# The first 128 positions of a sparse attention, computed on 64-key ranges, with the division on GpSimd

## The chip, the cores and the metric

The kernel runs on one core of a Trainium2 chip. Its engines work side by side and each in its own order: TensorE (PE, matrix products and transposes; PEld is its loading of weights), VectorE (DVE), ScalarE (ACT), GpSimd (POOL) and SyncE (SP). SP, ACT and POOL can issue DMA transfers, which 16 DMA engines carry out. Sums of PE land in PSUM, which has eight banks; all else is in SBUF. The metric is the time of one execution on the device in microseconds, the median of several runs.

## The reference

```python
# q, k, v: (4, 8, 576, 64)
scores = scale * np.matmul(q, k.transpose(0, 1, 3, 2))
rel = pos[:, None] - pos[None, :]
mask_local = (rel >= 0) & (rel < 32)
mask_strided = (rel >= 0) & (pos[None, :] % 32 == pos[:, None] % 32)
# heads 0 to 3 take mask_local, heads 4 to 7 mask_strided
attn = softmax(np.where(mask, scores, -1e9))        # sum + 1e-9 in the divisor
x = (attn @ v).transpose(0, 2, 1, 3).reshape(2304, 512)
h = np.maximum(x @ w_in, 0.0)                        # w_in (512, 2048)
x = (s * h * h + b) @ w_out                          # w_out (2048, 512)
out = ((x @ w_a) * (x @ w_b)) @ w_o2                 # d_ff 1536
```

The weights arrive as 64-bit floats. The kernel reads them as pairs of 32-bit words, builds 32-bit floats from them, and splits each into a high and a low half for PE.

## The kernel before

The work is one attention and two MLPs. The 2304 tokens are taken in five blocks. Block 0 has the first 128 positions of all four batch entries, 512 columns; blocks 1 to 4 have the other positions of one batch entry each. For each block the first MLP runs through 16 slices of its inner width: `h_mm` (12 matmuls, written `h`) and, two slices later, `o_mm` (12 matmuls, `acc`). During block n the attention of block n + 1 is computed in small steps between the slices (`plan`, `attend`), in four `local` and two `strided` pieces.

The first positions have nothing to hide behind. The class `First` computes them for one batch entry each, and the string `ORDER` interleaves the steps of the four by hand. In a step's name the last digit is the batch entry. `Tq` and `Tk` transpose q and k (`fps`), `qe` and `ke` copy them out, `S` makes the scores (`fss`): for each head a full 128x128 product, with the mask added by a matmul. `m1`, `m0`, `nb`, `su`, `e1`, `e0`, `sm_` and `rc` make maxima, exponentials, sums and reciprocals. `P1`, `P0` transpose the probabilities (`fpp`), `p1`, `p0` copy them out, `V` multiplies with v (`fpo`), `no` divides, `X` transposes the result (`fpx`), and `hi` and `lo` split it into the two halves of x. The steps `c1`, `d0`, `d1`, `d2`, `ch`, `cl` convert the first two slices of `w_in`; the digit says which. `W` issues weight loads, and `I8` lets PE run eight matmuls of a filler, `lull` (as `idle(8)` does at the start).

PE's instructions are issued in the order of the program (`in_order`), and so are those of ACT and DVE in this part (`act`, `dve`). SP's queue has all loads but two: q and k of the four entries, v, the first weights, s and b, and then the q and k of the first local piece (`qk`, lines 281 to 285), of the strided ones (`sqk`) and so on. A load takes one of eight semaphores in turn, so it is issued when the load eight places before it has landed. Piece 0 of `local` starts at step -5, so its transposes (`pst`, line 291) stand on PE right ahead of the first `h`:

```python
if n == 1:
    near[0] = (0, near[0][1], (-5, -3, 0, 1, 1, 2, 3))
...
for number in (-5, -4, -3):
    attend(number)
```

GpSimd makes the masks: those of the first positions (`first_mask`, `fmask`) and those of the later pieces (`late_masks`, `mwork`).

Of the kernel before, what the change touches and what calls it, by code (L numbers as in the profile page):

```python
# [8 lines left out]
F32 = mybir.dt.float32  # L9
F32R = mybir.dt.float32r  # L10
U32 = mybir.dt.uint32
BF16 = mybir.dt.bfloat16
# [6 lines left out]
P = 128  # L19
# [6 lines left out]
def sparse_attention_two_mlps(  # L26
# [44 lines left out]
    ps_acc = ctx.enter_context(tc.tile_pool(name="ps_acc", bufs=4, space=PSUM))  # L71
    ps_h = ctx.enter_context(tc.tile_pool(name="ps_h", bufs=1, space=PSUM))
    ps_a = ctx.enter_context(tc.tile_pool(name="ps_a", bufs=3, space=PSUM))

# [478 lines left out]

    def slot(pool, shape, name, dtype=F32):
        return pool.tile(shape, dtype, tag="w", name=name)

    def first_mask():
        m = slot(wpa, [P, 2 * TF + TF], "fmask")
        m_b = m[:, 2 * TF:].bitcast(BF16)
        m = m[:, 0:2 * TF].rearrange("p (i c) -> p i c", i=2)  # L560
# [3 lines left out]
        nc.gpsimd.affine_select(  # L564
            out=m[:, 0], in_=m[:, 0], compare_op=ALU.is_ge, fill=NEG, base=0,
            pattern=[[-1, TF]], channel_multiplier=1,
        )
        nc.gpsimd.affine_select(
            out=m[:, 0], in_=m[:, 0], compare_op=ALU.is_gt, fill=NEG, base=STR,
            pattern=[[1, TF]], channel_multiplier=-1,  # L570
        )
        for i in range(TF // STR):
            nc.gpsimd.affine_select(
                out=m[:, 1], in_=m[:, 1], compare_op=ALU.not_equal, fill=0.0, base=-i * STR,
                pattern=[[-1, TF]], channel_multiplier=1,
            )
        m_b = m_b.rearrange("p (i c) -> p i c", i=2)
        nc.vector.tensor_copy(out=m_b, in_=m)
        return m_b
# [3 lines left out]

    def idle(number):
        for _ in range(number):
# [17 lines left out]

    class First:
        def __init__(self, bb, qk, vn, m_b, pool, tag):
            self.bb, self.qk, self.vn, self.m_b = bb, qk, vn, m_b
            self.bank = lambda shape, name: pool.tile(shape, F32, tag=tag, name=name)
            self.ps = {}

        def columns(self, e):  # L610
            if e == 0:
                self.qkT = slot(wpb, [P, 2, HP, TF], "fqkT")
            ps = self.ps["T", e] = self.bank([P, HP, TF], "fps")
            for pair in range(HP):
                mm_t(ps[:, pair], self.qk[:, e, 2 * pair:2 * pair + 2].rearrange("p h d -> p (h d)"), ident)
# [10 lines left out]
        def ke(self):  # L626
            if self.bb % 2:
                act(out=self.qkT[:, 1], in_=self.ps["T", 1], func=AF.Copy)
            else:
                dve("tensor_copy", out=self.qkT[:, 1], in_=self.ps["T", 1])  # L630

        def S(self):
            self.pt = slot(wpa, [P, 2, HP, TF], "fpt")
            self.mx = lp.tile([P, 2, HP], F32, tag="fmx", name="mx", bufs=2)
            self.sm = lp.tile([P, 2, HP], F32, tag="fsm", name="sm", bufs=4)
            for a in (1, 0):
                ps = self.ps["S", a] = self.bank([P, HP, TF], "fss")
                mm(
                    ps.rearrange("p (i j) c -> p i j c", i=2), lhsT=ident_b,
                    rhs=self.m_b[:, :, None, :].to_broadcast([P, 2, HP // 2, TF]), start=True, stop=False,  # L640
                )
            for pair in range(HP):
                for a in range(2):
                    qT, kT = (self.qkT[a * D:(a + 1) * D, e, pair] for e in range(2))
                    mm(self.ps["S", a][:, pair], lhsT=qT, rhs=kT, start=False, stop=(pair == HP - 1))

        def top(self, a):
            dve("tensor_reduce", out=self.mx[:, a], in_=self.ps["S", a], op=ALU.max, axis=AX.X)

        def m1(self):  # L650
            self.top(1)

        def m0(self):
            self.top(0)

        def nb(self):
            dve("tensor_scalar_mul", out=self.mx[:, 1], in0=self.mx[:, 1], scalar1=-scale)

        def su(self):
            dve(  # L660
                "tensor_tensor", out=self.pt[:, 0], in0=self.ps["S", 0],
                in1=self.mx[:, 0, :, None].to_broadcast([P, HP, TF]), op=ALU.subtract,
            )

        def e1(self):
            for pair in range(HP):
                act(
                    out=self.pt[:, 1, pair], in_=self.ps["S", 1][:, pair], func=AF.Exp, scale=scale,
                    bias=self.mx[:, 1, pair:pair + 1], accum_out=self.sm[:, 1, pair:pair + 1],
                )  # L670

        def e0(self):
            act(out=self.pt[:, 0], in_=self.pt[:, 0], func=AF.Exp, scale=scale)

        def sm_(self):
            dve("tensor_reduce", out=self.sm[:, 0], in_=self.pt[:, 0], op=ALU.add, axis=AX.X)
# [5 lines left out]
        def rows(self, a):  # L682
            if not hasattr(self, "pT"):
                self.pT = slot(wpa, [P, 2, HP, TF], "fpT")
            ps = self.ps["P", a] = self.bank([P, HP, TF], "fpp")
            for pair in range(HP):
                mm_t(ps[:, pair], self.pt[:, a, pair], ident)

        def P1(self):
            self.rows(1)  # L690

        def P0(self):
            self.rows(0)

        def p1(self):
            act(out=self.pT[:, 1], in_=self.ps["P", 1], func=AF.Copy)

        def p0(self):
            act(out=self.pT[:, 0], in_=self.ps["P", 0], func=AF.Copy)

        def V(self):
            self.po = self.bank([P, HP, 2, D], "fpo")
            for pair in range(HP):
                for a in range(2):
                    mm(
                        self.po[:, pair, a], lhsT=self.pT[:, a, pair], rhs=self.vn[:, 2 * pair + a],
                        start=True, stop=True,
                    )

        def no(self):  # L710
            self.xn = slot(wpb, [P, HP, 2, D], "fxn")
            r = self.sm.rearrange("p a r -> p r a")[:, :, :, None].to_broadcast([P, HP, 2, D])
            dve("tensor_tensor", out=self.xn, in0=self.po, in1=r, op=ALU.mult)

        def X(self):
            self.px = self.bank([P, HP, TF], "fpx")
            for pair in range(HP):
                mm_t(self.px[:, pair], self.xn[:, pair].rearrange("p a d -> p (a d)"), ident)
# [4 lines left out]
        def hi(self):  # L723
            act(out=self.part(0), in_=self.px, func=AF.Copy)

        def lo(self):
            dve("tensor_tensor", out=self.part(1), in0=self.px, in1=self.part(0).bitcast(F32), op=ALU.subtract)
# [306 lines left out]
    def next_weights(number):  # L1034
# [17 lines left out]
    for bb in range(B):  # L1052
        if bb % 2 == 0:
            vf = slot(wpb, [P, 2, H, D], "fv")
        vs.append(vf[:, bb % 2])
        qks.append(slot(wpb, [P, 2, H, D], "fqk"))
# [14 lines left out]
    banks = ((ps_acc, "acc"), (ps_a, "a"), (ps_acc, "acc"), (ps_a, "a"))  # L1071
    firsts = [First(bb, qks[bb], vs[bb], m_b, *banks[bb]) for bb in range(B)]
    pieces = [Piece(words[i], wpa) for i in range(AHEAD1)]
    lull = ps_h.tile([P, 3 * P], F32, tag="h", name="lull")
    idle(8)
    for what in ORDER.split():
# [8 lines left out]
        in_order(step) if name in ("Tq", "Tk", "S", "P1", "P0", "V", "X") else step()  # L1085
    for f, piece in enumerate(pieces):
        wi[f] = by_rows(piece.w)
    later = [Stream(convert_w2(), 3 * NF2 + 1, sum(T1[1:-1]) * NF1 - 3 * T1[-2])]
# [227 lines left out]
```

## Time and profile before

| | us |
|---|---|
| runs: lowest, median, highest | 900.24, 900.44, 900.62 |
| profiled execution: span, first to last instruction | 898.1 |
| median of the runs less that span | 2.3 |
| PE busy in the span | 888.6 |
| DVE, ACT, POOL busy | 620.5, 401.4, 42.0 |
| first `h` in the chain of waits | 31.78 |

The span is that of one execution under the profiler, and the time of a run has some 2 us around it. PE is busy nearly all of the span, but a busy PE isn't one at its peak, and in the first 60 us the chain of waits goes through all three other compute engines too. In the chain a line gives the start, the length, and the engine and tile that the end was waiting for; "x8" is eight instructions taken together. A timeline gives start, length, engine, line, operation, output<-input and shapes, and in brackets idle time ahead of the first. An fp32 matmul leaves two records, so 16 matmuls are "x32".

### The profile page before, as it was taken

To read this page: it belongs to the slowest core of one execution; us is meant where nothing else is said; L and a number is where in the kernel's file an instruction comes from. 1 tells how busy PE (TensorE), PEld (TensorE's weight loads), DVE (VectorE), ACT (ScalarE), POOL (GpSimd) and SP (SyncE) were. 2 spreads that over 40 slices of the span, in tenths; PEclk is the share of its full clock that TensorE was granted. 3 is DMA by queue.
4 is the path that set the end of the run, shared out by engine and by line. 5 is a ranking of instruction groups with operands and counts; after the bars stand their busy time and mean duration, and the time that the engine had idled before them with its cause. 6 is when DMAs were issued, how large, how long until landed. Compare 5 with 4: busy or idle time off the path is not lost.

```text
span 898.1 us, 16348 instructions
## 1 busy us (share of the span) xinstructions
PE 888.6 (99%) x6166; PEld 793.8 (88%) x6166; DVE 620.5 (69%) x1263; ACT 401.4 (45%) x866; POOL 42.0 (5%) x120
## 2 busy tenths in 40 slices
PE   8999999999999999999999999999999999999997
PEld 6778889999888899998889999988999988999986
DVE  6898995676766777727665777765776765776741
ACT  6777774434333343353333445354334444333322
POOL 6000000000000010001100000000000000000000
PEclk9999999999999999999999999999999999999999
DMA  9965534656765666446666343423432221433010
GB/s 229 292 204 162 166 77 134 159 149 162 207 170 159 176 190 172 130 137 220 196 214 207 129 141 112 138 80 113 151 99 94 84 94 59 124 95 106 30 36 35
DMA packets 156606, 126.41 MB, mean 141 GB/s; under 512 B 102256, under 2 KB 131440, under 8 KB 156528
## 3 DMA queue, kind: packets, MB, share of 16 engines
q1 hardware_dynamic: 149840, 109.12, 43.3%
q0 software_dynamic: 4608, 15.73, 4.4%
q8 instruction: 48, 0.79, 0.4%
q10 hardware_dynamic: 2080, 0.52, 0.3%
q14 instruction: 30, 0.25, 0.1%
HBM read 100.17 MB, written 25.17 MB: 140 GB/s over the span
## 4 chain that ended last, share of the span: by engine, by line
PE 97%; ACT 2%; DVE 1%; issue 0%; POOL 0%; ACTq 0%; POOLq 0%
PE acc L94 38%; PE pp L94 29%; PE h L94 22%; PE po L94 2%; PE pss L94 1%; PE ppt L97 1%; PE fpo L94 1%; PE fps L97 0%; PE lull L94 0%; ACT raw L130 0%; ACT fpt L596 0%; PE fss L94 0%; PE pst L97 0%; PE fpp L97 0%; PE fpx L97 0%; ACT r L778 0%
## 5 line engine op out<-in xcount | busy, mean ns | idle before, releaser
L94 PE MATMUL pp<-x2w,wf 128*128 128x384 f32 x1512 | 265.8, 335 | 0.0
L94 PEld LDWEIGHTS pp<-x2w,wf 128*128 128x128 f32 x1512 | 263.0, 188 | 1.8 <-ACT u L596 0.4
L94 PE MATMUL h<-x,w 128*128 128x512 f32 (+1 forms) x960 | 217.0, 374 | 0.0
L94 PE MATMUL acc<-gt,w 128*128 128x512 f32 (+2 forms) x960 | 210.7, 368 | 1.0 <-ACT w L111 1.0
L94 PEld LDWEIGHTS acc<-gt,w 128*128 128x128 f32 x960 | 175.5, 188 | 24.1 <-ACT w L111 1.5
L94 PEld LDWEIGHTS h<-x,w 128*128 128x128 f32 x960 | 171.8, 188 | 24.2 <-DVE w L112 0.5
L94 PE MATMUL acc<-o2w,abt 128*128 128x512 f32 x648 | 150.5, 390 | 0.0
L94 PEld LDWEIGHTS acc<-o2w,abt 128*128 128x128 f32 x648 | 121.4, 188 | 24.6
L778 ACT ACTIVATE r<-h 128x512 f32<-128x512 f32 (+1 forms) x80 | 44.4, 554 | 153.2 <-PE h L94 144.4
L788 DVE TENSOR_TENSOR r<-r 128x384 f32<-128x384 f32 (+1 forms) x64 | 40.0, 625 | 91.2 <-ACT gt L785 91.1
L601 DVE TENSOR_TENSOR u<-pp,u 128x384 f32<-128x384 f32 x72 | 39.9, 555 | 64.8 <-PE pp L94 59.3
L596 ACT ACTIVATE u<-pp 128x384 f32<-128x384 f32 x36 | 17.7, 493 | 115.6 <-PE pp L94 115.6
L596 ACT ACTIVATE wf<-w2t 128x512 fp32r<-128x512 f32 x72 | 45.2, 628 | 21.2 <-PE pp L94 20.3
L601 DVE TENSOR_TENSOR wf<-w2t,wf 128x512 fp32r<-128x512 f32 x72 | 49.3, 685 | 0.3 <-ACT wf L596 0.3
L130 ACT ACTIVATE raw<-raw 128x512 f32<-128x512 f32 x66 | 42.7, 671 | 8.2 <-DMA raw<-in_moe_w_a_dram 6.6
L136 DVE SCALAR_TENSOR_TENSOR raw<-raw 128x512 uint32<-128x512 uint32 x66 | 44.4, 689 | 0.7
L789 DVE TENSOR_TENSOR gt<-r,gt 128x384 fp32r<-128x384 f32 (+1 forms) x64 | 40.0, 624 | 3.6
L601 DVE TENSOR_TENSOR wf<-w2r,wf 128x512 fp32r<-128x512 f32 x72 | 39.6, 549 | 0.0
L596 ACT ACTIVATE wf<-w2r 128x512 fp32r<-128x512 f32 x72 | 37.2, 517 | 4.5 <-PE pp L94 4.0
L601 DVE TENSOR_TENSOR abt<-dly,abt 128x384 fp32r<-128x384 f32 x36 | 19.8, 556 | 25.0 <-ACT abt L596 24.9
L596 ACT ACTIVATE abt<-c 128x384 fp32r<-128x384 f32 x36 | 18.9, 524 | 40.4 <-DVE c L601 40.4
L785 ACT ACTIVATE gt<-r 128x384 fp32r<-128x384 f32 (+1 forms) x64 | 36.5, 571 | 0.4
(149 smaller groups left out, 805.1 us busy)
## 6 DMA issues: line engine op xcount, KB each, us to landing
w2t<-w2s SPq DMA_DIRECT2D x36, 512.0 KB
w2r<-w2d SPq DMA_DIRECT2D x60, 256.0 KB
raw<-in_moe_w_out_dram SPq DMA_DIRECT2D x28, 512.0 KB
w2d<-w2s POOLq DMA_DIRECT2D x36, 256.0 KB, 4.3
raw<-in_moe_w_in_dram SPq DMA_DIRECT2D x16, 512.0 KB
raw<-in_moe_w_a_dram SPq DMA_DIRECT2D x12, 512.0 KB
raw<-in_moe_w_b_dram SPq DMA_DIRECT2D x12, 512.0 KB
w2s<-w2t POOLq DMA_DIRECT2D x12, 512.0 KB, 4.0
```

What stands on the lines that cost most here:

```text
L94: last_pe[:] = [nc.tensor.matmul(*args, **kwargs).ins]
L97: last_pe[:] = [nc.tensor.transpose(*args).ins]
L130: nc.scalar.activation(out=high.bitcast(F32), in_=high.bitcast(F32), func=AF.Copy, scale=HIGH_SCALE)
L136: nc.vector.scalar_tensor_tensor(out=low, in0=high, scalar=3, in1=low, op0=ALU.logical_shift_left, op1=ALU.bitwise_or)
L596: i = nc.scalar.activation(**kwargs).ins
L601: i = getattr(nc.vector, method)(**kwargs).ins
L778: relu = nc.scalar.activation(out=r, in_=ph, func=AF.Relu)
L785: nc.scalar.activation(out=hi, in_=r, func=AF.Square)
L788: nc.vector.tensor_tensor(out=r, in0=r, in1=r, op=ALU.mult)
L789: last = nc.vector.tensor_tensor(out=lo, in0=r, in1=hi.bitcast(F32), op=ALU.subtract)
```

## The change

Only the first positions are changed, and with them the mask, the loads of v, the division, and `ORDER`.

The scores of a query block of 32 are made against 64 keys only: for the local heads the range of 64 that holds the 32 allowed ones, and for the strided heads the 64 keys of the same parity. So a row of probabilities has 64 numbers for a head instead of 128, and the two heads of a pair lie side by side in 128 columns: one transpose for both. One reduction takes all maxima, one exponential all heads. GpSimd divides the probabilities by their sums, before the transposes. The product with v gives x with its features on the partitions, so that the transposes of the result go away. v is loaded in windows of 64 rows: for each batch entry four loads for local heads (64x3x64) and two for strided ones (64x2x128) instead of one of 128x8x64. The scores get four PSUM banks of their own (`ps_first`), which `ps_acc` takes over afterwards.

```diff
     def first_mask():
...
-        for i in range(TF // STR):
+        for p0, p1, shift in ((0, WF, 0), (WF, WF + STR, STR), (WF + STR, P, STR)):
+            rel = dict(out=m[p0:p1, 0], in_=m[p0:p1, 0], fill=NEG)
             nc.gpsimd.affine_select(
...
+        for p0 in range(0, P, WF):
+            for i in range(TF // STR):
+                nc.gpsimd.affine_select(
+                    out=m[p0:p0 + WF, 1], in_=m[p0:p0 + WF, 1], compare_op=ALU.not_equal, fill=0.0,
...
+    def first_values(vn, bb):
+        for a in range(2):
+            rows = slice(a * WF, (a + 1) * WF)
+            for pair in range(HL // 2):
+                at = v[bb, 2 * pair + a]
+                nc.sync.dma_start(
+                    out=vn[rows, 0:3, pair], in_=bass.AP(at.tensor, at.offset, [[D, WF], [STR * D, 3], [1, D]])
+                )
+            at = v[bb, HL + a]
+            nc.sync.dma_start(
+                out=vn[rows, 3:5].rearrange("r q g d -> r q (g d)"),
+                in_=bass.AP(at.tensor, at.offset, [[2 * D, WF], [2 * S * D, 2], [1, 2 * D]]),
+            )
...
+    KE_ACT, NM_POOL = (1, 3), (0, 1, 2, 3)
...
         def S(self):
...
+                for j in range(TF // STR):
+                    for a in range(2):
+                        qT, kT = (self.qkT[a * D:(a + 1) * D, e, pair] for e in range(2))
+                        if pair < HL // 2:
+                            w0 = (0, 0, STR, WF)[j]
+                            lhsT, rhs = qT[:, j * STR:(j + 1) * STR], kT[:, w0:w0 + WF]
+                        else:
+                            g, u = divmod(j, 2)
+                            qT, kT = (t.rearrange("p (k g) -> p g k", g=2)[:, g] for t in (qT, kT))
+                            lhsT, rhs = qT[:, u * STR:(u + 1) * STR], kT
+                        mm(
+                            s_[j * STR:(j + 1) * STR, a, pair], lhsT=lhsT, rhs=rhs,
+                            start=False, stop=(pair == HP - 1),
+                        )
+
+        def mx_(self):
+            dve("tensor_reduce", out=self.mx, in_=self.s, op=ALU.max, axis=AX.X)
...
+        def ex(self):
+            flat = self.pt.rearrange("p q a c -> p (q a c)")
+            act(out=flat, in_=flat, func=AF.Exp, scale=scale)
...
+        def nm(self):
+            wide = self.sm[:, :, :, None].to_broadcast([P, HP, 2, WF])
+            if self.bb in NM_POOL:
+                nc.gpsimd.tensor_tensor(out=self.pt, in0=self.pt, in1=wide, op=ALU.mult)
...
         def V(self):
...
+                    if pair < HL // 2:
+                        for w, c in ((0, slice(0, WF)), (1, slice(WF, WF + STR)), (2, slice(WF + STR, TF))):
+                            mm(po[:, c], lhsT=self.vn[rows, w, pair], rhs=pT[:, c], start=True, stop=True)
+                    else:
+                        for g in range(2):
+                            mm(
+                                po.rearrange("p (k g) -> p g k", g=2)[:, g],
+                                lhsT=self.vn[rows, 3 + pair - HL // 2, g],
+                                rhs=pT[:, g * WF:(g + 1) * WF], start=True, stop=True,
+                            )
...
-        def X(self):
...
     ORDER = (
...
+        "Tq0 Tk0 Tq1 qe0 ke0 Tk1 S0 mx_0 qe1 ke1 S1 Tq2 su0 ex0 Tk2 mx_1 su1 qe2 ke2 ex1 Tk3 sm_0 sm_1 Tq3 S2 mx_2 "
+        "ke3 qe3 rc1 S3 c10 su2 mx_3 rc0 ex2 su3 nm1 sm_2 P1 ex3 nm0 rc2 nm2 P0 sm_3 d00 rc3 pe1 V1 d10 P2 d20 nm3 "
+        "pe0 hi1 pe2 P3 lo1 V0 W6 W7 ch0 pe3 V2 hi0 V3 d01 I8 hi2 cl0 hi3 lo0 lo2 lo3 c11 d11 d21 ch1 cl1"
     )
...
-        first_load(nc.sync, vs[bb], v, bb)
+        first_values(vs[bb], bb)
         if bb == 0:
             stage_next()
```

SP's queue, the loads between those of q and k and those of the local piece, before (`fv` is v, `raw` a weight as it comes, `sb` s and b, `qk` the q and k of the first local piece; a name's number is its buffer):

```order
L582 DMA fv_173<-in_v_dram 128x8x64
L118 DMA raw_188<-in_moe_w_in_dram 128x4x256
L582 DMA fv_173<-in_v_dram 128x8x64
L582 DMA fv_176<-in_v_dram 128x8x64 x2
L118 DMA raw_193<-in_moe_w_in_dram 128x4x256
L118 DMA raw_195<-in_moe_w_in_dram 128x4x256
L123 DMA raw_197<-in_moe_w_out_dram 128x1024
...
L283 DMA qk_591<-in_q_dram 128x2x64
L283 DMA qk_591<-in_k_dram 96x3x64
```

and now (for the values of the entries 1 and 2 the rows are like those of entry 3):

```order
L593 DMA fv_189<-in_v_dram 64x3x64 x2
L597 DMA fv_189<-in_v_dram 64x2x128
...
L120 DMA raw_211<-in_moe_w_in_dram 128x4x256
...
L593 DMA fv_195<-in_v_dram 64x3x64 x2
L597 DMA fv_195<-in_v_dram 64x2x128
L120 DMA raw_231<-in_moe_w_in_dram 128x4x256
L120 DMA raw_233<-in_moe_w_in_dram 128x4x256
L125 DMA raw_235<-in_moe_w_out_dram 128x1024
...
L285 DMA qk_698<-in_q_dram 128x2x64
L285 DMA qk_698<-in_k_dram 96x3x64
```

24 loads stand where four stood, six ahead of the first `raw` and eighteen ahead of the second; the weights and `qk` follow in the order that they had.

GpSimd's queue behind the late masks, now (`mwork` and `smask32` belong to the late masks, `fpt` holds the probabilities of one entry, `sm` their reciprocal sums):

```order
L214 AFFINE_SELECT mwork_274<-mwork_274 32x36 x15
L220 CAST smask32_156<-mwork_274 32x36 x4
L707 TENSOR_TENSOR fpt_384<-fpt_384,sm_386 128x512
L707 TENSOR_TENSOR fpt_343<-fpt_343,sm_345 128x512
L707 TENSOR_TENSOR fpt_453<-fpt_453,sm_455 128x512
L707 TENSOR_TENSOR fpt_496<-fpt_496,sm_498 128x512
L164 COPY x_2158<-x_950 128x8x64
```

The four divisions, of the entries 1, 0, 2 and 3, stand where before the copy of x followed the casts at once.

PE, the end of the first positions, now (the rest of V3, the filler, the local piece's transposes, the first `h`):

```order
L96 MATMUL fpo<-fpt,fv 64x64 x8
L96 LDWEIGHTS ident_b
L96 MATMUL lull<-ident_b 128x384
...
L99 MATMUL pst<-ident,qk 128x128 x2
L99 MATMUL pst<-ident,qk 128x96 x3
L96 MATMUL h<-x,w 128x512 x12
```

The 16 `fpx` transposes that stood ahead of the filler are gone; `pst` stands between the filler and `h`, as before.

## Rows read from the trace of the kernel before

**Rows 1.** The page, part 1: busy us (share of the span) x instructions.

```profile
PE 888.6 (99%) x6166; PEld 793.8 (88%) x6166; DVE 620.5 (69%) x1263; ACT 401.4 (45%) x866; POOL 42.0 (5%) x120
```

**Rows 2.** Chain of waits, 0 to 80 us: start us, us, what.

```profile
2.92 2.74 PE lull L94 x8
...
30.01 1.30 PE lull L94 x8
...
31.78 2.92 PE h L94 x12
...
42.70 0.68 DVE w L112
...
65.14 2.72 PE acc L94 x12
```

**Rows 3.** Timeline of SP's DMA issues, 0 to 40 us: start us, us, what.

```profile
0.81 2.20 SPq L582 DMA_DIRECT2D fqk<-in_q_dram  x3
...
8.75 1.14 SPq L582 DMA_DIRECT2D fv<-in_v_dram  x1
9.94 1.14 SPq L118 DMA_DIRECT2D raw<-in_moe_w_in_dram  x1
...
15.59 1.80 SPq L118 DMA_DIRECT2D raw<-in_moe_w_in_dram  x2
...
21.79 0.48 SPq L283 DMA_DIRECT2D qk<-in_k_dram  x1
...
24.57 0.32 SPq L283 DMA_DIRECT2D qk<-in_k_dram  x1
```

**Rows 4.** Waits of SP's queue, 0 to 35 us: total us, times, longest us.

```profile
SPq L283 <- DMA raw<-in_moe_w_in_dram: 1.2, 2, 1.0
...
SPq L283 <- DMA raw<-in_moe_w_out_dram: 0.9, 1, 0.9
```

**Rows 5.** Windows: busy us (x) by engine, granted clock, DMA share, GB/s.

```profile
2.00:3.00 1.00, 0.08 (x1) 0.08 (x2) 0.86 (x1) 0.91 (x1) 1.00 (x6) 1.00 0.56 130
...
3.00:12.00 9.00, 8.98 (x62) 6.31 (x64) 3.46 (x7) 3.46 (x13) 7.58 (x35) 1.00 1.37 226
...
20.00:26.00 6.00, 6.00 (x58) 6.00 (x56) 5.32 (x13) 5.32 (x17) 0.00 (x0) 1.00 1.05 355
...
28.00:29.00 1.00, 1.00 (x11) 0.86 (x10) 0.83 (x2) 0.39 (x1) 0.00 (x0) 1.00 0.48 111
```

**Rows 6.** Timeline of PE, 0 to 62 and 138 to 162 us.

```profile
31.15 0.63 PE L97 MATMUL pst<-ident,qk 128*128 128x128 f32 x5
...
139.20 0.46 PE L94 MATMUL pss<-qkT 64*32 64x64 f32 x32
...
154.15 0.67 PE L94 MATMUL po<-pT,vn 64*64 64x32 f32 x32
```

**Rows 7.** Groups on POOL by line: busy us, mean ns of one, idle before.

```profile
L212 POOL TENSOR_SCALAR_AFFINE_SELECT mwork<-mwork 64x72 f32<-64x72 f32 (+1 forms) x36 | 8.3, 232 | 2.1
L162 POOL CAST x<-x 128x512 fp32r<-128x512 f32 x2 | 1.5, 726 | 134.1 <-DMA o<-o1s 134.1
L217 POOL CAST lmask<-mwork 32x64 bf16<-32x64 f32 (+1 forms) x6 | 1.4, 240 | 0.2
```

**Rows 8.** Timeline of POOL, 0 to 62 us, its last row.

```profile
16.97 0.95 POOL L218 CAST smask<-mwork 32x36 bf16<-32x36 f32 x4
```

**Rows 9.** Issues of v loads by tile `vn`: duration ns min/median/max, first and last start.

```profile
L454 SPq DMA_DIRECT2D vn<-in_v_dram x48: 598/614/1372, 134.2 to 374.3; - x48
L298 SPq DMA_DIRECT2D vn<-in_v_dram x8: 328/464/681, 29.9 to 108.3; - x8
```

**Rows 10.** The end: timeline of PE from 885 us, and a window (columns of rows 5).

```profile
884.83 8.78 PE L94 MATMUL acc<-o2w,abt 128*128 128x512 f32 x38
...
897.00:898.10 1.10, 0.00 (x0) 0.00 (x0) 0.00 (x0) 0.00 (x0) 0.00 (x0) 0.93 0.00 0
```

More of the change, by code (lines that the diff above doesn't have):

```diff
@@ L641, in S @@
                 )
             for pair in range(HP):
[L643 to L654, printed above, removed]
@@ L656, in nb @@
-        def nb(self):
-            dve("tensor_scalar_mul", out=self.mx[:, 1], in0=self.mx[:, 1], scalar1=-scale)
+                for j in range(TF // STR):
+                    for a in range(2):
+                        qT, kT = (self.qkT[a * D:(a + 1) * D, e, pair] for e in range(2))
[9 more added lines that the diff above has]
+                            start=False, stop=(pair == HP - 1),
+                        )
@@ L698, in p0, with P @@
-        def p0(self):
-            act(out=self.pT[:, 0], in_=self.ps["P", 0], func=AF.Copy)
+        def nm(self):
[3 more added lines that the diff above has]
+            else:
+                dve("tensor_tensor", out=self.pt, in0=self.pt, in1=wide, op=ALU.mult)
+        def P(self):
+            ps = self.ps["P"] = self.bank("fpp")
+            for pair in range(HP):
+                mm_t(ps[:, pair], self.pt[:, pair].rearrange("p a c -> p (a c)"), ident)
@@ L701, in V, with pe @@
+        def pe(self):
+            act(out=self.pT, in_=self.ps["P"], func=AF.Copy)
         def V(self):
-            self.po = self.bank([P, HP, 2, D], "fpo")
+            self.po = self.bank("fpo")
             for pair in range(HP):
                 for a in range(2):
[L705 to L713, printed above, removed]
@@ L715, in X @@
-        def X(self):
-            self.px = self.bank([P, HP, TF], "fpx")
-            for pair in range(HP):
-                mm_t(self.px[:, pair], self.xn[:, pair].rearrange("p a d -> p (a d)"), ident)
+                    rows = slice(a * WF, (a + 1) * WF)
+                    po, pT = self.po[a * D:(a + 1) * D, pair], self.pT[rows, pair]
+                    if pair < HL // 2:
+                        for w, c in ((0, slice(0, WF)), (1, slice(WF, WF + STR)), (2, slice(WF + STR, TF))):
+                            mm(po[:, c], lhsT=self.vn[rows, w, pair], rhs=pT[:, c], start=True, stop=True)
+                    else:
+                        for g in range(2):
[3 more added lines that the diff above has]
+                                rhs=pT[:, g * WF:(g + 1) * WF], start=True, stop=True,
+                            )
@@ L723, in hi @@
         def hi(self):
[L724 removed]
+            act(out=self.part(0), in_=self.po, func=AF.Copy)
         def lo(self):
[L727 removed]
+            dve("tensor_tensor", out=self.part(1), in0=self.po, in1=self.part(0).bitcast(F32), op=ALU.subtract)
     class Piece:
@@ L1070, in sparse_attention_two_mlps @@
     late_masks()
-    banks = ((ps_acc, "acc"), (ps_a, "a"), (ps_acc, "acc"), (ps_a, "a"))
-    firsts = [First(bb, qks[bb], vs[bb], m_b, *banks[bb]) for bb in range(B)]
+    firsts = [First(bb, qks[bb], vs[bb], m_b) for bb in range(B)]
     pieces = [Piece(words[i], wpa) for i in range(AHEAD1)]
-    lull = ps_h.tile([P, 3 * P], F32, tag="h", name="lull")
     idle(8)
@@ L1084, in sparse_attention_two_mlps @@
         step = getattr((pieces if name in ("c1", "d0", "d1", "d2", "ch", "cl") else firsts)[of], name)
-        in_order(step) if name in ("Tq", "Tk", "S", "P1", "P0", "V", "X") else step()
+        in_order(step) if name in ("Tq", "Tk", "S", "P", "V") else step()
     for f, piece in enumerate(pieces):
         wi[f] = by_rows(piece.w)
+    start.close()
+    ps_acc = ctx.enter_context(tc.tile_pool(name="ps_acc", bufs=4, space=PSUM, reuse_waits="tile"))
     later = [Stream(convert_w2(), 3 * NF2 + 1, sum(T1[1:-1]) * NF1 - 3 * T1[-2])]
```

78 lines of the change are left out of this document (28 added, 50 removed), and 4 rows, old and new, of the table ORDER.

## The prediction

> **What bounds the kernel now.** Start with the page: PE is busy 99% of the span [rows 1], so a change in the first microseconds is worth only what it moves the point from which PE runs without a gap. The chain of waits gives that point. Up to 31.8 us it goes through the first positions; from `h` at 31.78 it alternates with ACT and DVE, which convert weights, and at 65 us it is PE alone [rows 2]. So the question is when the first `h` starts. It starts when PE's order lets it, and that order has two things ahead of it: the filler `lull`, and five transposes `pst` of the local block's q and k. Next comes SP's timeline, because these transposes need four `qk` loads. SP issues values and weights from 8.75 us on, and only behind them the `qk` loads, the second at 21.79 and the last at 24.57 [rows 3]. Three of them were held until an earlier weight load had landed: SP's list of waits names `w_in` twice and `w_out` once [rows 4]. Last come the windows: the DMA engines run full early on (share 1.37, then 1.05) and fall to 0.48 in 28 to 29 us [rows 5], so the `qk` loads are in at about 28.7, an estimate: when the traffic ahead of them is gone. `pst` starts at 31.15 [rows 6], so they have some 2.4 us to spare.
>
> **The change, part by part.** The profiled execution has a span of 898.1 us, and 2.3 us lie around it in the median of the runs, 900.44. I work out what the chain of the span gains or loses and add it to this median.
>
> *Scores, softmax, product with v.* PE, DVE and ACT lose work. Sixteen matmuls of the new scores' shape, 64x64 for 64x32 weights, took 0.46 us (32 records) [rows 6]; now 32 make a batch entry, so at most 0.9, and the masks halve. The product with v becomes 20 small matmuls for an entry: sixteen like them took 0.67 us with four corners of the array at work [rows 6], and here only two corners are, so 0.8 to 1.7 us, and I take 1.1. Half of the `fpp` transposes and all of `fpx` go; DVE drops a maximum pass, the negation and the division for each entry, ACT 16 exponentials with their sums and 4 evictions. If nothing else held `h`, this would be the gain, several microseconds. Something else does, so I cost it at nothing; rival 1 says what is left where that cover is gone.
>
> *Mask and division on GpSimd.* The mask takes 14 selects instead of 6. Selects of 36 and 72 columns average 0.232 us [rows 7], and one starts a little before the last has ended: the 8 more cost 1.2 us, at most 1.9. GpSimd works in order, and the four divisions stand behind all late masks, whose last casts end at 16.97 + 0.95 = 17.9 us [rows 8]: now 19.1. A division of 128x512 by a broadcast operand is not in this trace. The nearest row, a cast of 128x512 with one input, takes 0.726, and casts of 64 and 96 columns 0.240 [rows 7]: about 0.17 fixed and 0.55 for 512 elements. A second input that is read for as long again gives 1.28, which I take; 0.73 is the lower end, and 3 us the upper, twice the dearer one and some for DVE's traffic. Four end at 19.1 + 5.1 = 24.2. Then P3, its eviction and V0, V2, V3 follow to about 28.2, and the lower halves on DVE come last. One more wait is new there: `d01`, the first step on the second `w_in`, stands ahead of three of them, and that load is late (28.3, below). 28.3 + 0.4 + 0.6 + 3 x 0.6 = 31.1: x is whole at about 31.1 us. This alone would leave `h` where it was, within half a microsecond.
>
> *The values loads.* Here I expect the loss. Four loads of 128x8x64 become 24 of 64 partitions, all on SP's queue: six ahead of the first `w_in`, eighteen between it and the second, and so ahead of every `qk` load. The queue moves in order. What does an issue cost? The trace has almost the same transfer later: windows of 64 rows of v with a step of 32 rows, put into 64 partitions. Its issues take 0.614 us (median of 48, never under 0.598) [rows 9]; SP adds 0.05 between two (8.75 + 1.14 to 9.94 [rows 3]), so 0.66 from start to start. Windows of 96 rows take 0.464 [rows 9]. I take 0.66 for all 24, for the eight strided ones with some doubt; 0.46 is the low end. From 8.75 us on, 24 x 0.66 + 0.47 for the first `w_in` puts the second `w_in` at 25.1 instead of 15.59 [rows 3].
>
> That is 9.5 us at the issue, less at the landing: before, it was queued behind other bytes and landed at 21.8 (the second `qk` issue waited for it [rows 3, 4]); now the queue is nearly empty. 1.2 us to the first byte (the first load is issued at 0.81, traffic starts in 2 to 3 us [rows 3, 5]), 1.45 for 512 KB at 355 GB/s [rows 5] and some 0.6 to report make 28.3. Behind it everything repeats itself: the second, third and fourth `qk` load wait for the two `w_in` and the first `w_out` behind the values, and lie behind two more weights. Before, this took from 21.8 to 28.7, 6.9 us. So the last `qk` is in at 28.3 + 6.9 = 35.2, and `pst` starts then instead of at 31.15: **+4.1 us**. Behind `pst` on PE stands the whole MLP, and ACT's copy of `pst` is ahead of the first Relu. So what DVE and ACT gained early is not redeemed: from the end of the first `h` the chain runs through Relu, Square and conversions to the `w` at 42.70, which `acc` waits for [rows 2], and none of these can begin before. At most the one `w` step of 0.6 us that is now done early comes off; I take 0.
>
> *PE's clock.* The same filler of eight matmuls took 2.74 us at the start and 1.30 at 30 us [rows 2], so the first ran at 1.2 GHz and the second at 2.4. (The column of granted clocks shows 1.00 at 2 to 3 us too [rows 5], though that stretch was slow.) At the end PE stops at 884.83 + 8.78 = 893.6, and the clock falls only in 897 to 898.1, mean 0.93 [rows 10]. Now PE would be idle from the end of the filler, about 29.6, to 35.2, longer than these 4 us. If the clock is low at `pst`, a slow stretch of some 4 us, like the first, loses half of itself: 2.1 us. If V and the filler themselves run slow, they end later, PE idles less and the loss is nearer 0. I take **+1.0**, the middle. The Trainium skill ("TensorE: Matmul & The Clock Gate", "HAM oscillation — how this bites in real kernels") says that an idle wait between bursts of matmuls puts the array back to half clock, burst after burst; by that rule the term is the whole 2.1 us and the time 906.6. No row of this trace shows a fall between two bursts.
>
> Sum: 900.4 + 4.1 + 1.0 = **905.5 us**. Late next are the strided block's loads behind `qk` on SP; their transposes come after the first `acc`, so they have the time of four `h` and `acc` groups.
>
> **The rivals.**
> 1. *The issues are cheap.* If a values load issues within 0.49 us from start to start, `pst` is not late: 35.2 - 24 x (0.66 - 0.49) = 31.1. Below 0.46 the engines' rate binds, 0.26 MB more at 226 GB/s [rows 5], 1.2 us on 28.7, so 29.9. But x is whole only at 30 to 31, so `h` starts between 1.3 us earlier and as before: 899.1 to 900.5; with a cold start up to 901.5, with the 0.6 of `w` redeemed 898.5. For it: the eight strided loads have no row like them, and the 128- and 96-partition `qk` loads issue in 0.32 to 0.48 us [rows 3]. Against: sixteen have their like at 0.61 every time. Chance 0.27. A page has a price that would bring this about: the Trainium skill ("DMA: Bandwidth & Descriptors", "Why a DMA increments its semaphore by 16 and not by 1") gives 512 sequencer cycles for an issue on previous generations; at the 1.2 GHz of its TensorE page that is 0.43 us, an estimate, and the time would be about 900.3. The 0.61 of [rows 9] speaks against it.
> 2. *GpSimd ends last.* If a division takes 3 us, because its reads compete with DVE's, four end at 31.1 and x is whole at 35.5, `h` at about 36: 905 to 907. It decides from 2.9 us a division on. The cast's 0.73 speaks against it. Chance 0.09.
> 3. My forecast, the queue on SP: 0.64. Its own range is 902.5 to 908: 0.55 instead of 0.66 takes off 2.6 us, the clock moves it by 1.1 either way.
>
> **How the numbers follow.** About 0.2%, 1.8 us, is what a measurement of this kernel can tell from no change. Slower by more: the forecast and rival 2 nearly whole, 0.72. Within: most of rival 1, 0.19. Faster: its lower tail, 0.09. The range of 8 in 10 leaves out what lies below 899.0 and the few cases above 908.0.
>
> **What would show it.** Right: in SP's timeline, 24 issues of `fv` of 0.6 us each up to 25 us; DMA traffic well under 200 GB/s between 14 and 25 us; a gap of some 5 us on PE before `pst`, ended by the `qk` load; `h` at about 36; a second filler of 1.3 or 2.7 us, which tells the clock. The divisions on GpSimd start at about 19 us and take 1.3 each. Wrong: issues of 0.4 us, `pst` right behind the filler, and PE idle only ahead of the P transposes.

## The result, and the profile after

The changed kernel takes 913.47 us (median of 4 runs, 913.25 to 914.25) against 900.34 for the kernel before: ratio 1.0145, 95% interval 1.0133 to 1.0157. It is slower by 13.1 us; I had forecast 5.1, with 908.0 as the upper end of the range. The direction and the place were right, the size was not.

The page of the kernel after, parts 1 and 2 (the rows that answer to [rows 1], and the granted clock in 40 slices):

```profile
span 911.5 us, 16851 instructions
...
PE 887.9 (97%) x6422; PEld 793.0 (87%) x6422; DVE 615.2 (67%) x1251; ACT 394.8 (43%) x830; POOL 48.1 (5%) x132
...
PEclk9699999999999999999999999999999999999999
```

PE is busy as long as before (887.9 us against 888.6 [rows 1]), although DVE and ACT do less: the 13.4 us of longer span are time in which PE stood still or ran slowly, nearly all of it in the first 60 us. The chain of waits, 0 to 70 us, which answers to [rows 2]:

```profile
8.96 1.16 SPq L593
...
12.14 1.27 SPq L593
...
18.02 1.52 SPq L597
...
25.45 1.47 SPq L593
...
28.28 0.59 SPq L120
28.91 5.68 DMA raw<-in_moe_w_in_dram
34.61 6.16 DMA qk<-in_q_dram
40.90 1.14 PE pst L99 x5
42.04 3.80 PE h L96 x12
```

Before, this chain ran through PE from the first microseconds on. Now SP's queue is the chain from 9 to 29 us: lines 593 and 597 are the 24 v loads. Behind them come a weight load, a `qk` load, and only then `pst`. (The `raw` in these rows, landed at 34.61, is the third `w_in`, issued right behind the second; the third `qk` load was held until then.) The timelines of PE, after and before, give the ledger (start us, us, what, [idle before <- what ended it]). After:

```profile
21.77 2.12 PE L99 MATMUL fpp<-ident,fpt 128*128 128x128 f32 x8 [5.38 <-POOL fpt L707]
...
33.08 1.47 PE L96 MATMUL lull<-ident_b 128*128 128x384 bf16 x8
40.90 1.14 PE L99 MATMUL pst<-ident,qk 128*128 128x128 f32 x5 [6.35 <-DMA qk<-in_q_dram]
41.75 4.08 PE L96 MATMUL h<-x,w 128*128 128x512 f32 x12
...
54.27 4.62 PE L96 MATMUL acc<-gt,w 128*128 128x512 f32 x12 [2.10 <-ACT w L113]
58.73 0.60 PE L99 MATMUL ppt<-ident,lpt 128*96 128x128 f32 x4
```

Before:

```profile
31.56 3.12 PE L94 MATMUL h<-x,w 128*128 128x512 f32 x12
...
42.59 3.04 PE L94 MATMUL acc<-gt,w 128*128 128x512 f32 x12 [1.04 <-ACT w L111]
45.47 0.60 PE L97 MATMUL ppt<-ident,lpt 128*96 128x128 f32 x4
```

`pst` starts 9.75 us later (31.15 [rows 6]). The first `h` ends 11.15 later: 1.4 more, since `pst` and `h` take 1.14 and 4.08 us instead of 0.63 and 3.12. The first `acc` starts 11.7 later: the stall ahead of it is 1.06 longer, the two `h` before it are 0.52 shorter (24 matmuls in 5.74 us instead of 6.26). `ppt` behind it starts 13.26 later: 1.6 more, `acc` taking 4.62 instead of 3.04. From there the distance stays. The windows say why the same matmuls take longer (columns of [rows 5]):

```profile
20.30:30.00 9.70, 8.23 (x85) 7.17 (x87) 5.58 (x10) 4.03 (x8) 4.64 (x6) 0.50 0.35 79
28.00:29.00 1.00, 1.00 (x13) 0.69 (x12) 0.00 (x0) 1.00 (x3) 0.00 (x0) 0.50 0.24 53
30.60:34.50 3.90, 3.90 (x93) 3.11 (x88) 1.35 (x3) 2.36 (x4) 0.00 (x0) 1.00 1.01 361
37.40:44.00 6.60, 3.10 (x10) 2.68 (x11) 2.42 (x4) 1.96 (x4) 0.00 (x0) 0.50 0.76 164
...
54.40:57.70 3.30, 3.30 (x8) 2.65 (x9) 3.30 (x7) 2.36 (x5) 0.00 (x0) 0.50 0.98 313
```

The granted clock is 0.50, so 1.2 GHz, in three stretches, and 1.00 (2.4 GHz) between them. Ahead of each PE had stood: from 16.4 to 21.8, from 34.6 to 40.9, and for 2.1 us ahead of `acc`. Before, [rows 5] and [rows 10] show no such fall after the start.

GpSimd and DVE (timelines):

```profile
20.67 2.04 POOL L707 TENSOR_TENSOR fpt<-fpt,sm 128x512 f32<-128x512 f32 x2
...
24.91 1.31 POOL L707 TENSOR_TENSOR fpt<-fpt,sm 128x512 f32<-128x512 f32 x1 [0.74 <-DVE sm L620]
```
```profile
21.75 0.69 DVE L620 TENSOR_REDUCE sm<-fpt 128x8 f32<-128x512 f32 x1 [3.39 <-POOL fpt L707]
...
23.46 0.99 DVE L620 TENSOR_SCALAR raw<-raw 128x512 uint32<-128x512 uint32 x1
...
33.15 0.43 DVE L620 TENSOR_SCALAR raw<-raw 128x512 uint32<-128x512 uint32 x1 [5.31 <-DMA raw<-in_moe_w_in_dram]
...
34.10 1.88 DVE L620 TENSOR_TENSOR x<-fpo,x 128x512 fp32r<-128x512 f32 x3
```

The late masks end at 20.59 (17.92 before [rows 8]). The divisions start at 20.67 and take 1.02 to 1.31 us. x is whole at 34.10 + 1.88 = 36.0, not at 31.1, because `d01` waited 5.3 us for the second `w_in`. This lies hidden behind `pst` at 40.9, and became visible only in the experiments.

### The profile page after: what moved, and what is told of

It is laid out like the page before. It is cut to its first block, busy times and chain, and to the rows that moved or that the text cites. A ratio compares the mean times of both kernels' runs of the same rounds, so it can differ in the third digit from the quotient of the medians.

```text
span 911.5 us, 16851 instructions
## 1 busy us (share of the span) xinstructions
PE 887.9 (97%) x6422; PEld 793.0 (87%) x6422; DVE 615.2 (67%) x1251; ACT 394.8 (43%) x830; POOL 48.1 (5%) x132
## 4 chain that ended last, share of the span: by engine, by line
PE 94%; SPq 3%; ACT 1%; DMA 1%; issue 0%; DVE 0%; ACTq 0%
PE acc L96 38%; PE pp L96 29%; PE h L96 22%; PE po L96 2%; PE pss L96 1%; SPq L593 1%; PE ppt L99 1%; SPq L586 1%; DMA qk<-in_q_dram 1%; SPq L597 1%; DMA raw<-in_moe_w_in_dram 1%; PE pst L99 0%; ACT raw L132 0%; ACT w L113 0%; ACT r L794 0%
## 5 line engine op out<-in xcount | busy, mean ns | idle before, releaser
L620 DVE TENSOR_TENSOR abt<-dly,abt 128x384 fp32r<-128x384 f32 x36 | 19.9, 555 | 25.2 <-ACT abt L615 25.1
```

The source lines that it names most:

```text
L620: i = getattr(nc.vector, method)(**kwargs).ins
```

## The experiments

Theory A: the number of v loads on SP's queue sets when `pst` and x are ready. Theory B: GpSimd's divisions hold x, and the queue only covers it. Theory C: the clock that falls while PE waits costs a further 3 us. "After" is the changed kernel, 913.5; the kernel before ran beside each group at 900.2 to 900.4. The runs of one changed kernel lie up to 3.9 us apart, and a trace shows one of them.

**1. Moving what stands behind the v loads.** Three runs change only the order of issues on SP, a fourth only the engine of the division:

```
# e1: local q and k ahead of all v loads
-            near[0] = (0, near[0][1], (-5, -3, 0, 1, 1, 2, 3))
+            near[0] = (0, early, (-3, 0, 1, 1, 2, 3))
...
+    early = local(0, 1, 0, TF, 4)
+    next(early)
     for bb in range(B):
         first_values(vs[bb], bb)
# e2: the second w_in behind the first
         if bb == 0:
-            stage_next()
+            for _ in range(2):
+                stage_next()
...
# e3: e2, and early/next(early) there too
# e4
-    KE_ACT, NM_POOL = (1, 3), (0, 1, 2, 3)
+    KE_ACT, NM_POOL = (1, 3), ()
```

> The four q and k loads of the first local piece are issued on SP ahead of the 24 v loads; nothing else is moved. Theory A (SP's queue behind the narrow v loads sets when `pst` can start): these loads land long before 34.6 us, so `pst` starts right behind the filler matmuls at about 34.6 and waits for no load; the second w_in is issued about 2 us later than in the changed kernel (30 instead of 28.3), so x is whole at about 38 and the first h starts there instead of at 42.0. Time 913.5 - 4 - 1 (part of the slow clock) = 908.5 us, between 906 and 911. Theory B (x, held up by the divisions on GpSimd and the DVE work beside them, is the real bound and SP's queue only covers it): h still cannot start much before 38 to 40, 911 to 913.5.

> Only the second w_in is moved, from behind all v loads to right behind the first w_in; the local q and k loads stay where they are. Theory A: `d01` no longer waits on DVE and x is whole at about 33 instead of 36, but `pst` still waits for q and k, which land at about 40 (one weight load fewer is ahead of them in the last burst, so up to 1.5 us earlier); time 911.5 to 914. Theory B, in the form that x sets the first h: 909 to 911.

> The second w_in and the four local q and k loads are issued behind the v loads of the first entry, ahead of the v loads of the other three. Theory A: no wait of `pst` for a load, x whole at 34 to 36, first h there instead of at 42.0, and less slow clock behind it: 913.5 - 6.5 - 1.5 = 905.5 us, between 903.5 and 907.5. Theory B (GpSimd's divisions bound x): h not before 38, 909 us or more.

> All four divisions on DVE instead of GpSimd; loads as in the changed kernel. Theory A: the product of P and v and x come sooner or at the same time, but `pst` still waits for q and k until about 40.9: 912.5 to 914.5 us. Theory B: the divisions were the bound, 908 to 911 us.

Measured: e1 909.9 us (909.3 to 911.5), e2 913.9 (913.6 to 914.2), e3 909.9 (908.1 to 911.3), e4 912.3 (911.8 to 914.6). In e1 `pst` no longer waits for its loads, but for x, and x for the second `w_in`, as the chain shows; the first `h` starts at 37.0, 4.7 us earlier, of which 3.6 reach the end:

```profile
29.50 4.96 DMA raw<-in_moe_w_in_dram
35.42 1.88 DVE x L620 x3
```

In e2 the wait for q and k stays (5.87 us, `pst` at 40.31) and so does the time. In e3, where both are early, the next to be late is v itself, on PE's timeline:

```profile
32.31 1.16 PE L96 MATMUL fpo<-fpt,fv 64*64 64x64 f32 x22 [1.33 <-DMA fv<-in_v_dram]
34.18 0.84 PE L96 MATMUL fpo<-fpt,fv 64*64 64x64 f32 x12 [0.70 <-DMA fv<-in_v_dram]
```

So its first `h` came at 38.1, and not at 34 to 36: I had expected 905.5 and overlooked that the v loads of the last entry are then the end of the queue. By its numbers e3 is what theory B foretold for it (`h` not before 38, 909 or more); the trace has PE waiting for v, 2.0 us in all, in the last products. In these runs the load that stands last is the one waited for. e4 is 1.2 us under after, which its interval (1.0117 to 1.0151) does not tell from after's; its `pst` waits 9.5 us for `qk`, and theory B's 908 to 911 is not met.

**2. The number of loads, and the clock.** e5 loads v over 128 partitions, 8 loads instead of 24 with the same bytes in all (v's tile then holds other values than the product needs). e7 puts the 24 narrow loads into the kernel before and changes nothing else. e6 gives PE something to do while it waits.

```
# e5, in first_values, in place of its body
+        flat = vn.rearrange("p w g d -> p (w g) d")
+        first_load(nc.sync, flat[:, 0:H], v, bb)
+        nc.sync.dma_start(
+            out=flat[:, H:H + 2], in_=v[bb, 0:2, 0:TF, :].rearrange("h t d -> t h d")
+        )
# e7, in the kernel before
-        first_load(nc.sync, vs[bb], v, bb)
+        for a in range(2):
+            for h0, h1 in ((0, 3), (3, 6), (6, 8)):
+                rows = slice(a * (TF // 2), (a + 1) * (TF // 2))
+                nc.sync.dma_start(
+                    out=vs[bb][rows, h0:h1], in_=v[bb, h0:h1, rows, :].rearrange("h t d -> t h d")
+                )
# e6, in ORDER
-d01 I8 hi2
+d01 I8 I9 I9 I8 I4 hi2
```

> The changed kernel with v by 8 loads over 128 partitions (8 heads and 2 heads of each entry) instead of 24 over 64; the v tile then holds other values than the product needs, and all else is computed as before. Theory A (the number of loads in SP's queue): the second w_in is issued at about 16 instead of 28.3, the local q and k land at about 31 as in the kernel before, and `pst` no longer waits for them; then x, whole at about 34 as in the run with the second w_in moved, sets the first h. That is 8 us sooner than 42.0: 913.5 - 8 - 1.5 (slow clock) = 904 us, between 902.5 and 906. What is left over 900.4 is the price of theory B's chain (GpSimd's divisions and DVE's work beside them). If the loads' number did not matter: 911 or more.

> The kernel before, with v of the first positions by 24 loads over 64 partitions (6 per entry: two halves of the positions by three groups of heads) instead of 4 over 128; the same bytes into the same places, nothing else. Theory A: the second w_in is issued at about 28, the local q and k land at 39 to 41, `pst` 8 to 10 us later than 31.15, and with the slow clock behind it 900.4 + 9 + 2 = 911.5 us, between 908.5 and 914: most of the change's loss with nothing else of the change. Theory B (GpSimd): 904 us or less.

> The changed kernel with 38 filler matmuls instead of 8 ahead of `pst`, so that PE is busy from 33 to about 40 at its clock of then; loads and their wait as they are. Theory C (the granted clock that falls while PE waits costs 1.4 us in `pst` and the first h, and as much again in the first acc): the clock stays at 1.0 until the first h, `pst` still ends its wait at 40.9, 910.5 to 912.2 us. If the fall costs nothing: 913.5.

Measured: e5 906.6 us (904.9 to 907.5; ratio to before 1.0066, interval 1.0051 to 1.0081), e7 908.8 (907.2 to 911.0; 1.0095, 1.0078 to 1.0112), e6 910.4 (908.8 to 912.7). The v loads alone cost the kernel before 8.4 us, and fewer of them give the changed kernel 6.9 back. (e5's first `h` starts at 34.9, as expected; the time lies 0.6 over its range, with a mean granted clock of 0.62 from 22 to 33 us, in P and V, and again from 47.5 to 52, in the first `acc`.) SP's timeline of e7 (the run of 911.0 us) has the whole mechanism in three rows, and its PE timeline the consequence:

```profile
8.80 4.44 SPq L1064 DMA_DIRECT2D fv<-in_v_dram  x6
...
13.92 12.57 SPq L1064 DMA_DIRECT2D fv<-in_v_dram  x18
26.54 1.15 SPq L118 DMA_DIRECT2D raw<-in_moe_w_in_dram  x2
```
```profile
40.11 1.14 PE L97 MATMUL pst<-ident,qk 128*128 128x128 f32 x5 [0.73 <-DMA qk<-in_q_dram]
```

The second `w_in` is issued at 26.5 instead of 15.59 [rows 3], and `pst` starts at 40.1 instead of 31.15. Theory A stands, as the larger part. (Number and width of the loads change together in e5 and e7 and were not tried apart; after's chain shows the time in the issues, one behind the other.) In e6 the filler bridges the wait, and the clock stays up (windows of e6, the run of 908.8 us):

```profile
32.30:39.00 6.70, 6.48 (x38) 3.48 (x38) 5.13 (x9) 3.04 (x5) 0.00 (x0) 1.00 0.85 259
40.00:45.00 5.00, 5.00 (x37) 3.78 (x36) 0.83 (x4) 2.61 (x6) 0.00 (x0) 1.00 0.99 279
50.70:53.00 2.30, 2.30 (x10) 1.90 (x11) 2.30 (x5) 1.35 (x3) 0.00 (x0) 1.00 1.04 370
```

`h` takes 3.01 us and the first `acc` 3.02, and 30 matmuls that compute nothing save 3.1 us. That is theory C's 3.0 (1.4 + 1.6) in size, but only the first part is shown to be the filler's, `pst` and `h`. The first `acc` took 3.02 us in e4 too, which has no more filler than after; its stall was 1.53 us there and 1.55 in e6, instead of 2.10. Nor need all of the gain be the clock: in this run the second `w_in` was issued at 26.5 and `pst` started at 39.3, so the loads were in sooner than in the profile of after.

**3. What is left when v is out of the way.** e10 is e5 with the late masks behind the four divisions and four buffers for the sums (`sm`) instead of two, and the divisions held in their order; e14 is e5 with the four buffers alone.

```
# e14, and e10
-            self.sm = lp.tile([P, HP, 2], F32, tag="fsm", name="sm", bufs=2)
+            self.sm = lp.tile([P, HP, 2], F32, tag="fsm", name="sm", bufs=4)
# e10 besides (last_nm is the last division)
-    late_masks()
     firsts = [First(bb, qks[bb], vs[bb], m_b) for bb in range(B)]
...
+    with after(list(last_nm)):
+        late_masks()
     start.close()
```

> The run with v by 8 wide loads (v's tile again with other values than the product needs), and besides the late masks behind the divisions and four buffers for the sums. Theory B as a second bound: the divisions begin at 16.5 instead of 20.8, PE's wait of 6 us ahead of the first P transposes shrinks to about 1.5, its clock does not fall there, x is whole at about 31 and `pst` at 31 (q and k land), first h at about 31.5 to 32.5: 906.6 - 3 = 903.6 us, between 902 and 905. If masks ahead of the divisions cost nothing: 906 or more.

> The run with v by 8 wide loads (v's tile with other values than the product needs) with four buffers for the sums instead of two, the late masks left ahead of the divisions. If the masks ahead of the divisions were the second bound, the divisions still begin at 20.7 and the time is within 1 us of that run's 906.6; if the wait for the two buffers was it, 904 or less, near the 902.6 of the run with both changed.

Measured: e10 902.6 us (901.0 to 904.9, ten runs; 1.0025, 1.0015 to 1.0034), e14 906.8. The buffers alone show no gain (906.6 without them); the masks in front of the divisions cost 4 us once the queue no longer covers them, through PE's wait and the slow clock behind it. PE ahead of the first P transposes, first e14, then e10:

```profile
22.78 2.11 PE L99 MATMUL fpp<-ident,fpt 128*128 128x128 f32 x8 [7.01 <-POOL fpt L700]
```
```profile
17.25 0.66 PE L99 MATMUL fpp<-ident,fpt 128*128 128x128 f32 x4 [1.21 <-POOL fpt L701]
```

So theory B holds as a second bound, and by its place: the division is not dear, it stands behind some 15 us of mask work. In e10 `pst` waits for `qk` again (2.65 us), with the first `h` at 32.0.

e5 and e14 together show that the price in clock is not fixed. The first `acc` waits as long in both, and the granted clock is 0.50 in the one (47.6 to 50.5 us) and 1.00 in the other (47.3 to 50.2). First e5, then e14:

```profile
47.56 4.57 PE L96 MATMUL acc<-gt,w 128*128 128x512 f32 x12 [3.35 <-ACT w L113]
```
```profile
47.26 3.07 PE L96 MATMUL acc<-gt,w 128*128 128x512 f32 x12 [3.37 <-ACT w L113]
```

**4. The full computation with both taken out.** e8 moves v of entry 3 to ScalarE's queue and the second `w_in` and the local q and k ahead of v of entries 0 and 2, with e10's edits but for the wide loads. e9 has v of entries 2 and 3 on GpSimd's queue, those edits, and the order below; in e9d the divisions are on DVE instead, and the masks are not held back. e11 to e13 move those loads once more: entry 2's to behind the smaller mask set, entry 3's to SP (e11), to GpSimd right behind entry 2's (e12), or between GpSimd's third and fourth division (e13).

```
# e9, the issues (on SP where no engine is named)
+    first_values(vs[2], 2, nc.gpsimd)
+    first_values(vs[3], 3, nc.gpsimd)
+    first_values(vs[1], 1, nc.sync)
+    stage_next()
+    first_values(vs[0], 0, nc.sync)
+    stage_next()
+    early = local(0, 1, 0, TF, 4)
+    next(early)
...
# e9, in ORDER
-rc1 S3 c10 su2 mx_3 rc0 ex2 su3 nm1 sm_2 P1 ex3 nm0
+rc1 S3 su2 mx_3 rc0 ex2 su3 nm1 sm_2 P1 ex3 c10 nm0
-V3 d01 I8 hi2 cl0 hi3 lo0 lo2 lo3 c11 d11 d21 ch1 cl1
+V3 c11 d01 cl0 lo0 I8 hi2 d11 hi3 lo2 d21 lo3 ch1 cl1
```

> The changed kernel with v of entry 1 first, then both w_in, then the local q and k, then v of entries 0 and 2 on SP; v of entry 3 issued by ScalarE where it waited for the first w_in; the divisions on GpSimd ahead of the late masks; four buffers for the sums. Theory A with the second bound taken out too: `pst` waits for no load, x is whole at 30 to 32, first h at 32 to 33, no long gap of PE: 900 to 903 us. If something else holds x (DVE or ScalarE), the first h comes at 34 or later: 903.5 us or more.

> The changed kernel with the 12 v loads of entries 2 and 3 issued by GpSimd (0.54 us for a load there later in the kernel), which does its late masks only behind the four divisions; SP then has 12 v loads with the first w_in between the two entries, the second w_in and the local q and k behind them; four buffers for the sums; the conversion of the second w_in ahead of the last two entries' x. Theory A plus the second bound (masks ahead of the divisions) both taken out: divisions begin at about 16.5 instead of 20.7, q and k land before 27, x whole at 28 to 30, first h at 29 to 31 (31.8 in the kernel before), PE's gaps short: 897.5 to 901 us. If a third thing bounds (DVE's or ScalarE's chain, or GpSimd's loads): first h at 33 or later, 902.5 us or more.

> As the run with v loads on GpSimd, but the divisions on DVE and the late masks left where the scheduler puts them. Theory: DVE is the busiest engine between 9 and 30 us and takes 4 divisions of 0.68 us more (2.7 us), but isn't slowed by GpSimd's divisions; within 1 us of the run with the divisions on GpSimd, at 898 to 902 us. If GpSimd's divisions as such were the bound: 2 us or more below that run.

> As the run with v loads on GpSimd, but only entry 2's six loads are there, behind the smaller of the two late mask sets (so from about 10 to 14 us, when q and k of entry 3 have nearly landed); entry 3's six stand on SP behind the local q and k. If the collision of GpSimd's v loads with q and k of entries 2 and 3 (PE waited 3.7 us for k at 12 to 15.6) was what kept that run at 902.3: q and k of entry 3 land by 13, divisions begin at about 16.5, x whole at 28 to 29.5, first h at 29 to 30: 897.5 to 900.5 us. If SP's six loads of entry 3 are late (landing after 28): first h at 31 or later, 900 to 902. If the collision was not the cause: 902 or more.

> As the run before it, with entry 3's six v loads on GpSimd too, behind entry 2's (from about 10 to 18 us). SP is freer by 4 us, so w_out and the later weights are issued at 20 instead of 24, but the first division waits for GpSimd's loads, until about 17.8 instead of 16.5: first h within 1 us of the other run's, 898 to 901 us. If the issue of weights bounds the stage behind the first h: 1 us or more below the other run.

> As the run with entry 2's v loads on GpSimd behind the small mask set, but entry 3's six loads go to GpSimd too, between its third and fourth division, instead of to SP behind the local q and k. SP then issues the third and later weights about 4 us sooner (w_in at 22 instead of 26.8, and the one whose landing ended the wait of 4.1 us ahead of the first acc at about 33 instead of 37). Theory D (what is left of the loss is SP's queue again, now through the weights behind the v loads): first h at 31 to 32, the wait ahead of the first acc back to 1 to 1.7 us, acc at 42.5 to 43.5: 900 to 901.5 us. If the weights' issue were not it: 902.5 to 904, as before.

e8 took 925.7 us, far from 900 to 903. ScalarE held x, as the other branch of the expectation allows, but for a reason that I had not thought of. ScalarE's list of waits has 26 us without a computation, and the chain shows what the last of its loads waited for:

```profile
ACT fpt L615 <- DMA fv<-in_v_dram: 26.0, 1, 26.0
```
```profile
32.85 7.35 DMA sqk<-in_k_dram
40.23 0.60 ACTq L597
```

The last of ScalarE's six loads was issued when a strided `k` load of SP had landed, and SP had issued that one behind v and the weights; the exponentials behind it on ScalarE waited as well. This fits loads of both queues that take the same eight semaphores in turn. The trace does not show semaphores by number, so that reading is argued.

e9 took 902.3 us (901.4 to 904.0, ten runs; 1.0024, 1.0015 to 1.0034), the best with the whole computation: 11.1 us under after, and still 2.2 over before, short of the 897.5 to 901 expected. Its first `h` came at 33.1. PE had waited early, ahead of the transposes of entry 3:

```profile
15.64 1.94 PE L99 MATMUL fps<-ident,fqk 128*128 128x128 f32 x8 [3.69 <-DMA fqk<-in_k_dram]
```

In after this wait was 1.19 us. e11 was to test whether the v loads on GpSimd compete with q and k of the same entries: with those loads later its wait for k was 1.72 us, its first `h` started at 31.0, half a microsecond earlier than in the kernel before, and its time was 903.0 (901.5 to 903.9), as slow as e9. So the wait answered, and the time is that of "not the cause". What was gained was lost again 13 us later on PE:

```profile
31.02 3.00 PE L97 MATMUL h<-x,w 128*128 128x512 f32 x12
...
44.46 4.49 PE L97 MATMUL acc<-gt,w 128*128 128x512 f32 x12 [4.10 <-ACT w L114]
```

ACT had waited 2.5 us for a `w_in` load that SP issued at 37.1, behind the v loads and everything after them, and the slow clock followed. e13, made to see whether that was the queue, shrank the wait to 1.55 us, but the six loads between the divisions put the last division at 24.84 instead of 21.83, and from 20.8 to 34 us the granted clock was 0.50 (V0, V2 and V3 6.94 us instead of 4.36): first `h` at 35.75, 904.0 us. (The clock had begun to fall before the first of the six loads, at 21.19: its mean from 20.0 to 20.8 is 0.76. So the slow stretch is not shown to be their doing.) So the wait answered as theory D said and the time did not. e12 took 904.3 (first `h` at 35.3, the first division later than meant). e9d took 907.6 but says nothing of the division: loads had slipped between the selects of the first mask, and PE's scores waited 6.45 us for it. Whether GpSimd's division as such costs or gains something is therefore left open; e4's 1.2 us do not settle it. No version beat the kernel before.

## Why the prediction was wrong in size

- *Where it would show*: right. 24 issues of mostly 0.61 us, DMA at 79 GB/s between 20 and 30 us, a gap ahead of `pst` ended by a `qk` load, divisions of 1.02 to 1.31 us. Rival 1 (cheap issues) and rival 2 in its form (3 us a division) fell: none of the 24 issues took less than 0.605 us, so neither 0.49 nor the 0.43 named beside rival 1 occurred.
- *The failed step* is the **+4.1 us** of the section on the values loads: it measured +9.75. Three sizes in it were too small. The second `w_in` was issued at 28.28, not 25.1: four of the 24 issues took 1.16 to 1.52 us, 3.0 us more than four of 0.61. I had seen such an issue in [rows 9], whose longest is 1.372, and taken the median for all. (Their number varies: in e6's trace two of the same 24 issues took over 1 us, and the second `w_in` went out at 26.5.) It landed at 33.1 (the end of `d01`'s wait), 4.9 us after its issue, where I had built 3.2 from an empty queue. The queue was nearly empty (53 GB/s from 28 to 29 us); but 1.1 MB moved until it landed (229 GB/s from 28.28 to 33.1), twice its size, and four more weight loads were issued by 31.2. That they shared the engines with it is likely and was not tried. From there to `pst` 7.75 us passed, where [rows 3] and [rows 5] had given 6.9. 3.2 + 1.65 + 0.85 = 5.7, the difference from the 4.05 that I had rounded to 4.1.
- *PE's clock*: forecast +1.0, measured some 3. I costed one fall, ahead of `pst`, and took the middle of 0 to 2.1. That one cost 1.4. The other 1.6 came 12 us later, in the first `acc`, behind a stall of 2.1 us that had been 1.0 before. The Trainium skill ("TensorE: Matmul & The Clock Gate", "HAM oscillation — how this bites in real kernels") tells of a kernel whose array goes back to half clock at every wait between its bursts. Three rows of windows here agree, and my reading that no row of before did was no reason to halve the price. But not every wait did it: e14's of 3.37 us left the clock at 1.00, so part of this price differs from run to run.
- *x whole at 31.1, hidden*: hidden, but at 36.0. I added `d01`'s wait with the second `w_in` at 28.3; it came at 33.1. I did not see the wait of `sm` for its two buffers (3.39 us on DVE); e14 shows no cost of it beside wide loads.
- *Mask and division*: the eight more selects moved the end of the late masks by 2.7 us, where I had 1.2, so the divisions began at 20.67 and not at 19.1. Their place behind the late masks was seen, its price not, since it was counted only up to "x is whole". e10 puts it at 4 us when the queue is short.
- *Scores, softmax and product costed at nothing*: no run contradicts it. In e11 the first `h` began half a microsecond earlier than before, and nothing of that reached the end.

## What to carry to other kernels

Before work is made smaller by splitting a load, count the new loads on the queue that issues them and follow every load behind them to its reader, not only the first: here q and k, a weight, v's own last piece and later weights were each the bound in turn. Cost a queue with its long issues, not with its median, and set aside a price in clock for each new gap on TensorE, as a range: the same gap cost 1.5 us in one run and nothing in another. A unit that looks idle may still have a long list in front of the new work; its place in that list counts for more than its duration.

## What the hardware showed that I had not expected

- An issue of a 64-partition load took 0.61 us on SP nearly always, and 1.16 to 1.52 in four of 24; GpSimd's issues of the same loads took 0.59 to 0.80. Fewer, wider loads were not cheap each: e5's eight took 0.47 to 1.82 us. What makes an issue long was not tried.
- The granted clock fell to 0.50 after PE's waits of 5.4 and 6.35 us, and in the first `acc` behind one of 2.1 us; with fillers (e6) it stayed at 1.00 from the second of these places on. A wait alone does not foretell it: behind 3.35 us it was 0.50 in e5, behind 3.37 it was 1.00 in e14, ahead of the same `acc`. What tells them apart was not found.
- While GpSimd divided, DVE's shift of 128x512 took 0.99 us; in the same trace it takes 0.43 when GpSimd rests. The two coincide; it was not tried alone.
